# Where the weight steps of one attention turn stand in its written order, and when the last held-back bias rows are stored

## The chip, the cores and the metric

The kernel runs on one core of a Trainium2 chip. The metric is the device time of one execution in microseconds; before the change it is 788.43 us, the median of three runs.

## The reference

Attention with a learned relative-position bias feeds a Fourier mixing layer and a dense layer. Shapes: batch 4, 8 heads, 576 positions, head size 64; model width 512, hidden width 2048.

```python
scores = q @ k.T / sqrt(64) + bias                    # bias: per head, 576 x 576, from a small MLP
attn   = exp(scores - max) / (sum + 1e-9)
x      = concat_heads(attn @ v)                       # [4, 576, 512]
u      = x + real(fft2(x))                            # over positions and width
un     = (u - mean) / sqrt(var + 1e-6)
out    = u + relu(un @ w_ch1) @ w_ch2                 # 512 -> 2048 -> 512
```

## The kernel before

**Stages.** The first stage (about 66 us) computes the bias rows, in 36 steps `u` of 16 rows for all heads, and the scores of attention unit 0. A unit is a pair of heads of one batch element; there are 16. Fifteen turns follow, `turn_of(n, between)` (L530), called from the loop at L579; then a hand-written tail (TAIL, L65), the mixing and the dense layers.

**A turn.** In a turn of about 16 us TensorE computes the scores of unit n while unit n-1 is transposed and multiplied with its values. The order of a turn is written by hand as a list of words (ORDER, L49; SECOND, L57, for n = 1 alone). `S4` is a score block on TensorE (L272), `D4` adds the bias on VectorE and keeps the row extremes (L290), `X4` is the exponential on ScalarE (L298). `T10` and `R1` are transposes on TensorE (L441, L431 to L436), `VT10` and `VR1` copy them from PSUM (L421 on ScalarE or L423 on VectorE), `A0` to `A4` multiply with the values (L462), `Q0` and `Q1` make the reciprocals, `E` and `Y` turn the result back and scale it. A stroke counts back one unit. Turn 0 executes no word, since unit 0 was scored in the first stage and there is no earlier unit. The loop has `tc.manual_schedule` for TensorE, VectorE and ScalarE (L545): these three execute their words in exactly the written order. GpSimd and the DMA queue of SyncE (SP) are ordered by a planner, by program order and by the readiness that it works out for itself.

**PSUM.** Score blocks rotate through 2 buffers (`sps`, L413), so a new `S` waits for the `D` two blocks back. Transposes rotate through 2 buffers (`tps`, L410), so a `T` waits for the copy `V` two transposes back.

**Weight steps.** In every turn from n = 1 on, `weights(n)` (L546) fetches one piece of each dense weight matrix and repacks it from 64-bit float to 32-bit float. The fetches `raw<-m` (L162) are issued on SP as `weights(n)` is called, each when its one buffer is free. Then `W0` and `U0` are ScalarE copies (L164), `W1` to `W3` and `U1` to `U3` are VectorE integer operations (L165 to L167), and behind `W3` and `U3` a store to DRAM is issued on SP (L552, L553). In SECOND these words stand in the second half: `U0` and `W0` ahead of `X6`, `W1` to `W3` behind it, `U1` behind `D8`, `U2 U3` close to the end.

**Held-back rows.** `bias_evac` (L332) writes bias rows into the buffer `ring` and, for every four steps (a group of 64 rows), stores heads 0 and 1 into the tiles that unit 0 reads (L346, L247 to L250). The other six heads go to DRAM by `keep_bias` (L326), six issues at L330, one group later: the list `later` holds back one group while the next is made. `while later: keep_bias()` (L591) stores what is left, at the end of turn 0; by the code that is one group, the last, six issues. Right behind it the tile `x` takes the buffer of `ring` (L593). From turn 3 on the rows come back as `bias<-bias_d` and `bias_r<-bias_d` (L234).

**Other work of a turn.** `prep(n+1)` (L198) splits the next unit's q and k on GpSimd, eight pieces placed behind the words 4, 12, ..., 60 of the list; `load(n+2)` (L183) fetches the unit after it on SP.

```python
rawp, rawu: one buffer "raw" each           # a fetch waits for the last reader of the one before
if len(later) > 1: keep_bias()              # L350, in bias_evac
for i, w in enumerate(SECOND if n == 1 else ORDER):   # L532
```

Of the kernel before, what the change touches and what calls it, by code (L numbers as in the profile page):

```python
# [54 lines left out]


SECOND = """  # L57
S1 D1 S2 T10' D2 S4 T00' VT10' T01' D4 VT00' VT01' S8' S3 T11' VT11' D8' X8' T02' D3 S6 Q0' VT02' D6 S0 R1'
R0' VR1' X3 VR0' D0 S7 S8 U0 T13' T12' W0 A0' D7 X6 W1 VT13' W2 W3 S5 T04' VT12' T03' D8 U1 Q1' A1' X7 X0
VT03' VT04' X1 D5 U2 U3 X5 A2'  # L60
""".split()


# [69 lines left out]
def body(ctx, tc, a, out):  # L133
# [49 lines left out]
    def load(n):  # L183
        hp, b = units[n]
        t = []
        for nm, w in (("qT", 2 * S), ("kT", KW)):
            f = ldp.tile([P, w], F32, tag=nm, name=nm)
            for e in range(2):
                nc.sync.dma_start(f[64 * e:64 * e + 64], a[nm][hp, b])
            t.append(f)  # L190
        ld[n] = t
# [6 lines left out]
    def prep(n):  # L198
        q, k = ld.pop(n)
        qs = stp.tile([P, 2 * S], F32R, tag="qs", name="qs")  # L200
        kh = stp.tile([P, KW], F32R, tag="kh", name="kh")
        kl = stp.tile([P, KW], F32R, tag="kl", name="kl")
        stk[n] = (qs, kh, kl)

        def hi(dst, src, c):
            if n < 2:
                nc.scalar.activation(dst[:, c], src[:, c], AF.Copy)
            else:
                nc.gpsimd.tensor_scalar(dst[:, c], src[:, c], 1.0, 0.0, ALU.mult, ALU.add)  # L209

        def lo(dst, src, ref, rows, c):
            eng = nc.vector if n < 2 else nc.gpsimd
            eng.tensor_tensor(dst[rows, c], src[rows, c], ref[rows, c].bitcast(F32), ALU.subtract)  # L213

        every, low = slice(0, 128), slice(64, 128)
        ca, cb, ck = slice(0, S), slice(S, 2 * S), slice(S, KW)
        return [
            lambda: hi(qs, q, ca), lambda: lo(qs, q, qs, low, ca),
            lambda: hi(kh, k, ca), lambda: lo(kl, k, kh, every, ca),
            lambda: hi(qs, q, cb), lambda: lo(qs, q, qs, low, cb),  # L220
            lambda: hi(kh, k, ck), lambda: lo(kl, k, kh, every, ck),
        ]
# [83 lines left out]
    with ExitStack() as st:  # L306
# [19 lines left out]
        def keep_bias():  # L326

            u, src = later.pop(0)
            for e in range(2, H):
                nc.sync.dma_start(bias_d[4 * (u - 3):4 * (u + 1), e], src[:, e])  # L330
# [74 lines left out]
    with ExitStack() as st:  # L405
# [124 lines left out]
        def turn_of(n, between):  # L530

            for i, w in enumerate(SECOND if n == 1 else ORDER):  # L532
                w, u = w.rstrip("'"), n - w.count("'")
                if w[0] in "WU":
                    if n:
                        wd(w)
                elif 0 <= u < U and (u or n == 1 or w[0] not in "SDX"):
                    steps[w[0]](u, w)
                for piece in between.pop(i, ()):
                    piece()  # L540
            assert not between
# [4 lines left out]
        def weights(n):  # L546

            wf = rawp.tile([P, 512], F32, tag="wf", name="wf")
            uf = rawu.tile([P, DM], F32, tag="wf", name="uf")
            w = widen(a["m1"][:, P * n:P * n + P].rearrange("(k p) c -> p k c", p=P), wf, [P, 4, P], rawp)  # L550
            u = widen(a["m2"][P * n:P * n + P], uf, [P, DM], rawu)
            w.append(lambda: nc.sync.dma_start(w1_d[n].rearrange("p k c -> p (k c)"), wf))  # L552
            u.append(lambda: nc.sync.dma_start(w2_d[n], uf))  # L553

            def step(name):
                todo = w if name[0] == "W" else u
                todo[int(name[1])]()
                if name[1] == "3":
                    todo[4]()
            return step  # L560

        def first_weights(i):

            c = slice(P * (i % 4), P * (i % 4) + P)
            wf = rawx.tile([P, P], F32, tag="wf", name="wx")
            if i < 4:
                res = widen(a["m1"][c, 0:P], wf, [P, P], rawx)
                dst = w1_d[0][:, i]
            else:
                res = widen(a["m2"][0:P, c], wf, [P, P], rawx)  # L570
                dst = w2_d[0][:, c]
            last = res.pop()

            def end():
                last()
                nc.sync.dma_start(dst, wf)
            return res + [end]

        for n in range(U - 1):  # L579
            pr = prep(n + 1) if n else []  # L580
            if n:
                wd = weights(n)
            between = {4 + 8 * i: [piece] for i, piece in enumerate(pr)}
            if n in FIRST:
                for i, piece in zip((10, 30, 40, 50), first_weights(FIRST.index(n))):
                    between[i] = [piece]
            turn_of(n, between)
            if n + 2 < U:
                load(n + 2)
            if n == 0:  # L590
                while later:  # L591
                    keep_bias()
                x = xp.tile([P, B, 5, DM], F32, tag="x", name="x")  # L593
            if n == 6:
                fs = tabp.tile([P, 3, 2, 2, NK], F32R, tag="tab", name="fs")
                nc.gpsimd.tensor_copy(fs[0:1, 0, 0, 0, 0:1], vt[6][0:1, 0, 0:1])
                nc.gpsimd.dma_start(fs, a["fs"])
# [197 lines left out]
        n = U - 1  # L795
# [146 lines left out]
        for b in range(B):  # L942
# [4 lines left out]
            if b + 1 < B:  # L947
                tl, un, pcs = prepare(b + 1)
                n = 4
            else:  # L950
                un, stats, scales = norm(rest_tiles)
                pcs = stats + scales
                n = 2
# [67 lines left out]
```

## Time and profile before

| | |
|---|---|
| three runs | 784.47, 788.43, 788.58 us; median 788.43 |
| the profiled execution | 784.86 us; its span in the trace 783.0 us |
| TensorE busy in the span | 758.1 us (97%) |
| VectorE, ScalarE, GpSimd busy | 433.7, 435.1, 354.1 us |
| mean granted TensorE clock | 0.99 of 2.4 GHz |

Times in the trace count from the first instruction. The second turn (n = 1) lies at 66 to 87 us, the third at 87 to 103 us. A line of a timeline has the start and the duration in us, the engine and the source line, what is written from what is read, and in brackets the idle time just before it with what ended it. Two instructions of one engine can overlap in the records, so the pitch, from one start to the next, is what one costs its engine. In the DMA queue's own timeline (SPq) the duration is that of the issue, not of the transfer.

### The profile page before, as it was taken

To read this page: it belongs to the slowest core of one execution; us is meant where nothing else is said; L and a number is where in the kernel's file an instruction comes from. 1 tells how busy PE (TensorE), PEld (TensorE's weight loads), DVE (VectorE), ACT (ScalarE), POOL (GpSimd) and SP (SyncE) were. 2 spreads that over 40 slices of the span, in tenths; PEclk is the share of its full clock that TensorE was granted. 3 is DMA by queue.
4 is the path that set the end of the run, shared out by engine and by line. 5 is a ranking of instruction groups with operands and counts; after the bars stand their busy time and mean duration, and the time that the engine had idled before them with its cause. 6 is when DMAs were issued, how large, how long until landed. Compare 5 with 4: busy or idle time off the path is not lost.

```text
span 783.0 us, 13209 instructions
## 1 busy us (share of the span) xinstructions
PE 758.1 (97%) x4786; PEld 617.4 (79%) x4786; DVE 433.7 (55%) x958; ACT 435.1 (56%) x898; POOL 354.1 (45%) x299
## 2 busy tenths in 40 slices
PE   6999899999999999979999999999999999999997
PEld 3567678887788877848888888888888888888896
DVE  7996787987877877587471232713237132111433
ACT  7995888788987888434333333334333342333453
POOL 0003556554663644256554434644355444445442
PEclk9999999999999999979999999999999999999999
DMA  8988989989879743631211121112211112111321
GB/s 220 238 222 228 254 235 297 298 227 283 243 204 284 204 135 92 208 110 28 66 32 50 43 94 54 40 41 64 72 54 41 41 54 95 43 53 54 119 90 61
DMA packets 59488, 103.16 MB, mean 132 GB/s; under 512 B 8768, under 2 KB 28864, under 8 KB 58304
## 3 DMA queue, kind: packets, MB, share of 16 engines
q1 hardware_dynamic: 58672, 98.99, 44.1%
q0 software_dynamic: 288, 3.02, 1.2%
q8 instruction: 37, 0.61, 0.3%
q10 hardware_dynamic: 464, 0.33, 0.1%
q14 instruction: 27, 0.22, 0.1%
HBM read 78.58 MB, written 21.07 MB: 127 GB/s over the span
## 4 chain that ended last, share of the span: by engine, by line
PE 88%; DVE 3%; ACT 3%; DMA 3%; SPq 2%; issue 1%; ACTq 0%; DVEq 0%
PE hp L898 25%; PE acc L912 25%; PE s L272 10%; PE o L462 10%; PE t L441 7%; PE bps L391 4%; PE zp L674 2%; PE abp L693 2%; DMA raw<-m 2%; SPq L330 1%; ACT p L298 1%; PE t L493 1%; DVE un L773 1%; PE ut L787 1%; PE t L431 1%
## 5 line engine op out<-in xcount | busy, mean ns | idle before, releaser
L904 DVE SCALAR_TENSOR_TENSOR hl<-hp,hh 128x512 fp32r<-128x512 f32 (+1 forms) x80 | 50.9, 636 | 229.4 <-ACT hh L903 229.4
L878 POOL TENSOR_TENSOR w1l<-w,w1h 128x512 fp32r<-128x512 f32 x80 | 105.8, 1323 | 106.1 <-ACT w1h L877 104.9
L878 POOL TENSOR_TENSOR w2l<-w2f,w2h 128x512 fp32r<-128x512 f32 x64 | 85.2, 1331 | 102.8 <-ACT w2h L877 102.5
L877 ACT ACTIVATE w1h<-w 128x512 fp32r<-128x512 f32 x80 | 50.4, 632 | 125.6 <-PE hp L898 110.2
L898 PE MATMUL hp<-uh,w1h 128*128 128x512 f32 (+1 forms) x320 | 118.7, 372 | 0.8 <-ACT uh L789 0.8
L898 PE MATMUL hp<-ul,w1h 128*128 128x512 f32 (+1 forms) x320 | 118.7, 371 | 0.7 <-DVE ul L790 0.7
L898 PE MATMUL hp<-uh,w1l 128*128 128x512 f32 (+1 forms) x320 | 118.5, 370 | 0.0
L290 DVE CUSTOM_DVE_ANT_0 p<-s,bias 128x576 f32<-128x576 f32 x128 | 95.1, 754 | 38.8 <-PE s L272 35.3
L877 ACT ACTIVATE w2h<-w2f 128x512 fp32r<-128x512 f32 x80 | 50.6, 632 | 117.8 <-POOL w1l L878 76.3
L912 PE MATMUL acc<-w2l,hh 128*128 128x512 f32 x288 | 112.4, 390 | 0.0
L912 PE MATMUL acc<-w2h,hh 128*128 128x512 f32 x288 | 111.9, 391 | 0.0
L912 PE MATMUL acc<-w2h,hl 128*128 128x512 f32 x288 | 107.4, 391 | 0.0
L272 PE MATMUL s<-kh,qs 128*128 128x288 f32 (+1 forms) x320 | 98.6, 327 | 1.9 <-DVE nm L290 1.8
L298 ACT ACTIVATE p<-p,nm 128x576 f32<-128x576 f32 x128 | 98.0, 772 | 2.8 <-DVE nm L290 1.6
L421 ACT ACTIVATE pt<-t 128x512 f32<-128x512 f32 x141 | 77.9, 594 | 35.9 <-PE t L441 20.0
L272 PE MATMUL s<-kl,qs 128*128 128x288 f32 (+1 forms) x320 | 88.2, 295 | 0.8 <-DVE kl L213 0.8
L462 PE MATMUL o<-pt,v 128*64 128x288 f32 x640 | 85.3, 412 | 0.0
L441 PE MATMUL t<-ident,p 128*128 128x128 f32 x576 | 80.4, 276 | 3.9 <-ACT pt L421 3.7
L209 POOL TENSOR_SCALAR kh<-kT 128x576 fp32r<-128x576 f32 (+1 forms) x28 | 22.8, 831 | 134.6 <-PE s L272 113.5
L272 PEld LDWEIGHTS s<-kh,qs 128*128 128x128 f32 (+1 forms) x320 | 58.4, 183 | 18.7 <-issue 7.0
L441 PEld LDWEIGHTS t<-ident,p 128*128 128x128 f32 x576 | 67.0, 142 | 7.3 <-ACT pt L421 4.8
L898 PEld LDWEIGHTS hp<-ul,w1h 128*128 128x128 f32 x320 | 60.8, 190 | 11.7 <-DVE ul L790 1.5
(136 smaller groups left out, 1387.1 us busy)
## 6 DMA issues: line engine op xcount, KB each, us to landing
w2f<-w_d SPq DMA_DIRECT2D x80, 256.0 KB, 2.6
raw<-m SPq DMA_DIRECT2D x30, 512.0 KB, 5.3
kT<-kT SPq DMA_DIRECT2D x32, 304.0 KB, 4.8
qT<-qT SPq DMA_DIRECT2D x32, 288.0 KB, 4.6
bias_d<-ring SPq DMA_DIRECT2D x54, 144.0 KB, 2.7
bias<-bias_d SPq DMA_DIRECT2D x24, 288.0 KB, 5.4
v<-v SPq DMA_DIRECT2D x16, 320.0 KB, 6.3
out<-x SPq DMA_DIRECT2D x18, 256.0 KB, 2.7
```

The lines of the kernel that those rows point to most:

```text
L272: nc.tensor.matmul(ps[:m, c, :CH], qs[:, c0:c0 + m], kk[:, k0 + c * CH:k0 + (c + 1) * CH], start=k == 0, stop=k == 1, skip_group_check=True)
L290: nc.vector.tensor_tensor_reduce(p, bank.pop((n, i))[:, :, :CH], bias, -0.125, 3.0e38, ALU.add, ALU.min, nms[n][:, blk:blk + 1])
L298: nc.scalar.activation(p, p, AF.Exp, bias=nms[n][:, blk:blk + 1], scale=-1.0, accum_out=sums[n][:, blk:blk + 1])
L391: nc.tensor.matmul(ps[32 * t4:32 * t4 + 32, c, :CH], w2[:, int(rev)], h[:, c * CH:(c + 1) * CH], start=True, stop=True, tile_position=(0, ...
L421: nc.scalar.activation(dst, src, AF.Copy)
L441: nc.tensor.transpose(tp[:, 128 * t:128 * t + 128], pb[t].rearrange("p h s -> p (h s)")[:, k0:k0 + 128], ident)
L462: nc.tensor.matmul(os_[u][e, c, :CH], vt[u][:, j, e], pts[u][:, 2 * j + h if j < 4 else 8, c * CH:(c + 1) * CH], start=j == 0, stop=j == 4 ...
L877: nc.scalar.activation(h, src, AF.Copy)
L878: eng.tensor_tensor(l, src, h.bitcast(F32), ALU.subtract)
L898: nc.tensor.matmul(ps[:, :N], (wh, wl)[wi][:, P * kb:P * kb + P], ut[ui][:, kb, :N], start=i == 0, stop=i == len(mm) - 1)
L904: nc.vector.scalar_tensor_tensor(hl[:, :N], ps[:, :N], 0.0, hh[:, :N].bitcast(F32), ALU.max, ALU.subtract)
L912: nc.tensor.matmul(acc[t], h[i][:, P * t:P * t + P], w[j], start=f == 0 and k == 0, stop=f == NF - 1 and k == 2)
```

## The change

Two edits. In SECOND the words W0 to W3 and U0 to U3 move to the end of the list, in the order W0 U0 W1 W2 W3 U1 U2 U3; all other words keep their order and the list its length of 62. The words W and U of ORDER, which all later turns use, stay. The second edit stores the held-back bias rows, and allocates `x`, at the end of turn 1, behind `load(3)`, and no longer at the end of turn 0.

```diff
 SECOND = """
-S1 D1 S2 T10' D2 S4 T00' VT10' T01' D4 VT00' VT01' S8' S3 T11' VT11' D8' X8' T02' D3 S6 Q0' VT02' D6 S0 R1'
-R0' VR1' X3 VR0' D0 S7 S8 U0 T13' T12' W0 A0' D7 X6 W1 VT13' W2 W3 S5 T04' VT12' T03' D8 U1 Q1' A1' X7 X0
-VT03' VT04' X1 D5 U2 U3 X5 A2'
+S1 D1 S2 T10' D2 S4 T00' VT10' T01' D4 VT00' VT01' S8' S3 T11' VT11' D8' X8' T02' D3 S6 Q0' VT02' D6 S0 R1' R0'
+VR1' X3 VR0' D0 S7 S8 T13' T12' A0' D7 X6 VT13' S5 T04' VT12' T03' D8 Q1' A1' X7 X0 VT03' VT04' X1 D5 X5 A2' W0
+U0 W1 W2 W3 U1 U2 U3
 """.split()
...
             if n + 2 < U:
                 load(n + 2)
-            if n == 0:
+            if n == 1:
                 while later:
                     keep_bias()
                 x = xp.tile([P, B, 5, DM], F32, tag="x", name="x")
```

## Rows read from the trace of the kernel before

**Rows 1.** The page: its first line, and the busy times of TensorE (with its weight loads), VectorE, ScalarE and GpSimd.
```profile
span 783.0 us, 13209 instructions
PE 758.1 (97%) x4786; PEld 617.4 (79%) x4786; DVE 433.7 (55%) x958; ACT 435.1 (56%) x898; POOL 354.1 (45%) x299
```

**Rows 2.** Who waited for whom on TensorE from 60 to 380 us, the row of the transposes: us in total, times, longest.
```profile
PE t L441 <- ACT pt L421: 3.7, 3, 2.9
```

**Rows 3.** The chain of waits from 55 to 122 us: start, us, what. The fetch of the weights, the copy that it releases, the value products of the second turn and third turn's first transposes.
```profile
74.02 5.49 DMA raw<-m
...
79.53 0.66 ACT uf L164
...
83.18 4.03 PE o L462 x32
...
89.65 0.44 PE t L441 x4
```

**Rows 4.** TensorE's timeline: T13' and T12' of the second turn, its T04' and T03', and T04' and T03' of the third turn.
```profile
76.23 1.04 PE L441 MATMUL t<-ident,p 128*128 128x128 f32 x8
...
82.03 1.14 PE L441 MATMUL t<-ident,p 128*128 128x128 f32 x8 [2.91 <-ACT pt L421]
...
97.79 1.04 PE L441 MATMUL t<-ident,p 128*128 128x128 f32 x8
```

**Rows 5.** ScalarE's timeline: VR0', U0, W0, then VT03' with VT04', and X8' of the third turn's list (behind X1 and X5); last U0, and VT13' with VT12', of the third turn.
```profile
74.68 0.60 ACT L421 ACTIVATE pt<-t 128x512 f32<-128x512 f32 x1 [0.32 <-PE t L431]
79.53 0.66 ACT L164 ACTIVATE uf<-raw 128x512 f32<-128x512 f32 x1 [4.25 <-DMA raw<-m]
80.09 0.65 ACT L164 ACTIVATE wf<-raw 128x512 f32<-128x512 f32 x1
...
83.87 1.08 ACT L421 ACTIVATE pt<-t 128x512 f32<-128x512 f32 x2
...
86.34 0.78 ACT L298 ACTIVATE p<-p,nm 128x576 f32<-128x576 f32 x1
...
94.27 0.65 ACT L164 ACTIVATE uf<-raw 128x512 f32<-128x512 f32 x1
...
96.16 1.07 ACT L421 ACTIVATE pt<-t 128x512 f32<-128x512 f32 x2
```

**Rows 6.** The SP queue's timeline: a bias row load of the fourth turn, the last stores of bias rows (two rows, 12 issues), the second turn's weight fetches, another early load, the store behind U3 and the third turn's fetch for U.
```profile
60.36 0.59 SPq L239 DMA_DIRECT2D bias<-bias_d  x1
...
62.76 4.22 SPq L330 DMA_DIRECT2D bias_d<-ring  x5
...
68.96 4.38 SPq L330 DMA_DIRECT2D bias_d<-ring  x7
73.46 1.12 SPq L162 DMA_DIRECT2D raw<-m  x2
74.62 0.55 SPq L247 DMA_DIRECT2D bias_r<-bias_d  x1
...
86.67 0.33 SPq L553 DMA_DIRECT2D w_d<-uf  x1
87.05 0.43 SPq L162 DMA_DIRECT2D raw<-m  x1
```

**Rows 7.** VectorE's timeline: W1, the D8 behind W3, U2, U3, and then D1 and VR1' of the third turn; last U1 and U3 of the third turn.
```profile
80.77 0.43 DVE L165 TENSOR_SCALAR raw<-raw 128x512 int32<-128x512 int32 x1 [4.61 <-ACT wf L164]
...
82.57 0.75 DVE L290 CUSTOM_DVE_ANT_0 p<-s,bias 128x576 f32<-128x576 f32 x1
...
84.85 0.69 DVE L166 SCALAR_TENSOR_TENSOR raw<-raw 128x512 int32<-128x512 int32 x1
85.58 1.07 DVE L167 SCALAR_TENSOR_TENSOR uf<-uf,raw 128x512 int32<-128x512 int32 x1
87.97 0.76 DVE L290 CUSTOM_DVE_ANT_0 p<-s,bias 128x576 f32<-128x576 f32 x1 [1.32 <-PE s L272]
...
88.66 0.45 DVE L423 COPY pt<-t 64x64 f32<-64x64 f32 x2
...
98.17 0.75 DVE L165 TENSOR_SCALAR raw<-raw 128x512 int32<-128x512 int32 x1
...
100.22 1.04 DVE L167 SCALAR_TENSOR_TENSOR uf<-uf,raw 128x512 int32<-128x512 int32 x1
```

**Rows 8.** GpSimd's timeline: the last pieces of `prep(2)`, and the first pieces of `prep(3)`.
```profile
76.58 2.78 POOL L213 TENSOR_TENSOR qs<-qT,qs 64x576 fp32r<-64x576 f32 x2
84.89 2.35 POOL L209 TENSOR_SCALAR kh<-kT 128x576 fp32r<-128x576 f32 x2 [5.53 <-DMA kT<-kT]
87.21 1.43 POOL L213 TENSOR_TENSOR kl<-kT,kh 128x576 fp32r<-128x576 f32 x1
```

**Rows 9.** The instructions on the tile `raw` in the whole span: ns min/median/max, first and last start, forms; and the time from the issue of a fetch to its landing.
```profile
L165 DVE TENSOR_SCALAR raw<-raw x38: 224/428/1030, 80.8 to 315.1; 128x512 int32<-128x512 int32 x30, 128x128 int32<-128x128 int32 x8
L166 DVE SCALAR_TENSOR_TENSOR raw<-raw x38: 277/693/1942, 81.2 to 317.5; 128x512 int32<-128x512 int32 x30, 128x128 int32<-128x128 int32 x8
...
L167 DVE SCALAR_TENSOR_TENSOR uf<-uf,raw x15: 691/702/1157, 85.6 to 318.2; 128x512 int32<-128x512 int32 x15
...
DMA to landing us min/median/max: 3.4/5.2/8.3
```

## The prediction

> **What bounds the kernel now.** The page comes first: TensorE is busy for 758.1 of 783.0 us [rows 1], so only a stretch in which it stands still can be shortened by a new order. The list of TensorE's waits says where one is: between 60 and 380 us the transposes waited three times for ScalarE's copies, 3.7 us in all, 2.9 us of it at once [rows 2]. TensorE's timeline puts that wait at T04' of the second turn, at 82.03 us, after 2.91 us idle [rows 4]. The chain of waits tells why: a weight fetch landed 5.49 us after 74.02 and released U0 on ScalarE [rows 3]. ScalarE had been idle for 4.25 us in front of U0, although VT13', for which T04' waits, stood behind it with its input ready: T13' and T12' ended by 77.27 [rows 4, 5]. The fetch was late because its issue, at 73.46, stood behind twelve stores of bias rows on SP [rows 6]. So the change aims at one place, and that place holds 2.91 us, 0.37% of the profiled execution.
>
> **Part 1, the words W and U at the end of SECOND.** What goes: U0 and W0 no longer stand in front of X6 and VT13'. ScalarE is free from 75.28 (74.68 + 0.60), does X6, and has both copies done before 78.1 (77.27 and two copies, 1.08 as a pair) [rows 4, 5]. TensorE reaches T04' at 79.12 (82.03 - 2.91), so nothing holds it there: minus 2.91 us at this point. The score buffers don't hold it either, because D7 and D8 no longer have a weight step ahead of them; `prep(2)` ends at 79.36 (76.58 + 2.78) [rows 8], some 5 us before its first use.
>
> What comes late next is VectorE, and here most of the gain is lost. Work forward from T04' at 79.12:
> - T04' and T03' take 1.14, to 80.26; ScalarE's VT03' then starts there and not at 83.87 [rows 5], 3.61 earlier. From VT03' to the end of X5 ScalarE has no gap (83.87 to 86.34), so X5 ends at 82.73. W0 starts there, U0 0.56 later (79.53 to 80.09), both done by 83.9.
> - On VectorE W1 starts 0.68 after W0 does (80.09 to 80.77), at 83.41. Three steps take 1.80 (W1 at 80.77, D8 behind W3 at 82.57) [rows 5, 7]; six take 3.60, to 87.01. D1 of the third turn stands behind them in the same queue, and VR1' behind D1: 0.69 (87.97 to 88.66) and 0.45. VR1' ends at 88.15.
> - T10' of the third turn needs the PSUM buffer that VR1' empties. In the chain of before it starts at 89.65, and from 82.03 to there TensorE is never idle [rows 3, 4]. It would be ready 2.91 earlier, at 86.74, but has to wait for 88.15. The gain left is 89.65 - 88.15 = 1.50 us; 1.4 us of standing still has moved over the turn's border.
>
> One term more: U1 to U3 now run at 85.2 to 87.0, beside the first pieces of `prep(3)`, on GpSimd from 84.89 [rows 8]. The nearest rows are the same steps beside such pieces. In the second turn U3 took 1.07 and not the 0.69 of the fastest; in the third, U1 took 0.75 where the median is 0.43, and U3 1.04 [rows 7, 9]. I charge U1 and U3, 0.32 + 0.35 = 0.67, since U2 kept its 0.69 in the second turn. What stands is a gain of 0.8 us. Bounds: if VectorE does not hold T10' at all, 2.9 us gained; with all six steps at the longest durations of the whole trace, 2 x (1.03 + 1.94 + 1.16) = 8.3 and not 3.6, 4.7 more, it is 3.2 us slower. I take the value near rows 7, because these are the same instructions beside the same GpSimd pieces; the longest ones are of some other stretch.
>
> The Trainium skill, page "SBUF — State Buffer", has a rule on which operations interfere: VectorE and GpSimd share one port pair as an exclusive lock, and the loser of a VectorE operation with two SBUF inputs and a GpSimd operation fully blocks. By it each of U1 to U3 could wait for a whole GpSimd operation. The trace so far shows 0.3 to 0.4 us lost at a meeting, less than a whole piece.
>
> The DMAs that move with these words: the stores behind W3 and U3, and with them the third turn's fetches, since each has one buffer. The fetch for U was issued at 87.05, 0.4 after U3 ended at 86.65 [rows 6, 7]. U3 now ends near 87.7, so the issue falls at 88.1; with the median landing of 5.2 [rows 9] the data is there at 93.3. The third turn's U0 stood at 94.27 without a wait [rows 5], and comes 0.8 earlier, at 93.5. That just fits: cost nothing, cover 0.2 us. Past that there is TensorE's own cover: T04' of the third turn needs VT13', started at 96.16, done by 96.7, and runs at 97.79 [rows 4, 5], which leaves 1.1 us more. The two small transfers behind Q1' leave SP earlier than before; nothing waits there. On GpSimd nothing is moved past: the same `prep(2)` pieces in the same sequence.
>
> **Part 2, the held-back rows.** The list holds one group by the code, not two, so six issues of 0.63 us (4.38 for seven) move, 3.8 us of SP time. The planner fills SP with what is ready: loads for the fourth turn stand at 60.36 and 74.62, far ahead of their place in the program [rows 6]. The held rows are ready when the first stage ends. So I expect the two fetches at about 69.6, behind the seventh store, with the six stores directly behind them, before 74.62. The fetches would land by 75.6 (5.5 each), but their first reader is W0 at 82.7: with part 1 in place an issue at 73.46, landing at 79.5, is early enough as well. So part 2 is worth nothing beside part 1; by itself, with the words where they were, it would have removed most of the 2.91 us. Bounds: 0, or 3.8 us of SP time if the stores come in front of the third turn's fetches.
>
> **The sum.** 784.86 (span 783.0 and 1.9 around it) - 0.8 + 0 = 784.1. The timed runs lie at two levels: one at 784.47, like the profiled execution, and two at 788.4 to 788.6. The median is of the upper level, 3.6 above the profiled one. I carry the difference over: 788.4 - 0.8 = 787.6 us.
>
> **Rivals.**
> - The wait comes back one turn later: the third turn's U0 waits for its fetch. From an issue at 88.1 it decides once the landing takes over 6.5 us (5.4 to U0, 1.1 to TensorE); the longest landing is 8.3 [rows 9], a stall of 1.8 and a net loss of 1.0: 785.9 in the profile, 789.4 as a median. Stores issued in front of it would do the same at 5.2. For it: the cover is only 0.2 + 1.1. Against it: the median, and the early loads of rows 6. This is the slower side.
> - VectorE's steps are blocked by whole GpSimd pieces: U1 to U3 wait out two pieces of kh and one of kl, 2.35 + 1.43 = 3.8 us [rows 8] in place of 0.67. T10' then starts at 91.9, 2.3 later than before: 787.1, or 790.7. Against it, rows 7. It is what the lock would do on the page "SBUF — State Buffer" of the Trainium skill.
> - VectorE holds nobody, because the six steps end by 85.6 (86.74 less D1 and VR1', 1.14): the full 2.9, 782.0 or 785.5. Against it: W1 can't start before W0, and six steps at 0.6 take 3.6.
> - The upper level is itself this wait: the executions at 788.5 would be those in which the fetch of rows 3 lands some 4 us later, as its range to 8.3 partly allows. Then the wait goes in all runs, and the median comes down to 784. For it: this fetch ends the longest of TensorE's waits on ScalarE. Against it: only an execution of the lower level is profiled, and other transfers could do it too.
> - Nothing changes (a gain of 0.3 or less), because some fetch or store further back sets the pace. Against it: TensorE leads the chain.
>
> **How the numbers follow.** Forecast, a gain of 0.3 to 1.5: 0.50. Wait one turn later 0.13, GpSimd 0.06, full gain 0.07, upper level gone 0.16, nothing 0.08. A difference of 0.5%, 3.9 us, is about what can be told from no change here, as the runs themselves spread over 4.1 us. No mechanism but the fourth rival moves the time by that much; the level on which the next median falls does. One of three runs was at the lower level, so a median there has a chance of about a quarter, and 784.5 - 0.8 = 783.7 then counts as faster. Together (0.16, and nearly a quarter of the rest that gains) 0.30 for faster; slower by that much needs a loss no rival reaches, 0.06; 0.64 for neither. The range goes from the lower level with the full gain, 784.5 - 2.9 = 781.6, to the upper level with the late fetch, 789.6.
>
> **What would show it.** Right: no wait of ScalarE in front of U0, T04' of the second turn near 79.1 without idle time, W0 near 82.7, six steps on VectorE in one piece to about 87.7, T10' of the third turn behind an idle time of 1.4 to 2.1 us that ends with VR1', the fetches at about 69.6. Wrong: an idle time in front of the third turn's U0 that reaches T04'; T10' without a wait; the stores issued behind 82 us; or a new difference behind 104 us, where no step of this working lies.

## The result: 0.63% slower, because a fetch of the third turn comes 6 us later

| | before | after |
|---|---|---|
| median of 8 runs each | 788.10 us | 792.01 us |
| lowest, highest | 784.47, 788.95 | 790.21, 794.37 |
| ratio after / before, of the means | | 1.0063 (95%: 1.0043 to 1.0083) |
| the profiled execution, its span | 784.86, 783.0 | 790.21, 788.4 |
| mean granted TensorE clock | 0.99 | 0.991 |

The page of after, its first line and its busy times, against [rows 1]:

```profile
span 788.4 us, 13208 instructions
...
PE 758.5 (96%) x4786; PEld 616.1 (78%) x4786; DVE 436.4 (55%) x958; ACT 434.8 (55%) x898; POOL 355.6 (45%) x299
```

The span grew by 5.4 us and TensorE's busy time by only 0.4. Who waited for whom on TensorE, 60 to 380 us, against [rows 2]:

```profile
PE t L441 <- ACT pt L421: 5.7, 3, 4.5
```

The same kind of wait, now 4.5 us at once in place of 2.9. TensorE's timeline of after says where, against [rows 4]; T04' of the second turn, T10', T13' and T04' of the third:

```profile
79.30 1.03 PE L441 MATMUL t<-ident,p 128*128 128x128 f32 x8
...
87.71 0.66 PE L441 MATMUL t<-ident,p 128*128 128x128 f32 x4 [0.90 <-ACT pt L421]
...
93.85 1.04 PE L441 MATMUL t<-ident,p 128*128 128x128 f32 x8
...
101.23 1.82 PE L441 MATMUL t<-ident,p 128*128 128x128 f32 x8 [4.49 <-ACT pt L421]
```

T04' of the second turn runs 2.73 us earlier and without idle time (82.03 before). T13' of the third turn is still 1.20 us ahead (95.05 before). Then T04' of the third turn is 3.44 us behind (97.79 before). ScalarE's timeline, against [rows 5], has the reason one step up: W0 and U0 of the second turn run where the order puts them, and U0 of the third waits 5.57 us for its fetch.

```profile
82.86 0.67 ACT L164 ACTIVATE wf<-raw 128x512 f32<-128x512 f32 x1
83.43 0.68 ACT L164 ACTIVATE uf<-raw 128x512 f32<-128x512 f32 x1
...
98.73 0.66 ACT L164 ACTIVATE uf<-raw 128x512 f32<-128x512 f32 x1 [5.57 <-DMA raw<-m]
```

The SP queue's timeline, against [rows 6]: the second turn's two fetches, the held-back stores, the store and fetch of W, then k of unit 4, and only then the store and fetch of U.

```profile
69.98 1.13 SPq L162 DMA_DIRECT2D raw<-m  x2
71.16 3.73 SPq L330 DMA_DIRECT2D bias_d<-ring  x6
...
85.48 0.34 SPq L552 DMA_DIRECT2D w_d<-wf  x1
85.86 0.43 SPq L162 DMA_DIRECT2D raw<-m  x1
91.40 1.11 SPq L189 DMA_DIRECT2D kT<-kT  x2
92.57 0.58 SPq L553 DMA_DIRECT2D w_d<-uf  x1
93.19 0.43 SPq L162 DMA_DIRECT2D raw<-m  x1
```

VectorE's timeline, against [rows 7]: W1, U3, D1 of the third turn, VR1'.

```profile
83.56 0.44 DVE L165 TENSOR_SCALAR raw<-raw 128x512 int32<-128x512 int32 x1 [3.30 <-ACT wf L164]
...
86.55 0.69 DVE L167 SCALAR_TENSOR_TENSOR uf<-uf,raw 128x512 int32<-128x512 int32 x1
87.16 0.75 DVE L290 CUSTOM_DVE_ANT_0 p<-s,bias 128x576 f32<-128x576 f32 x1
...
87.84 0.45 DVE L423 COPY pt<-t 64x64 f32<-64x64 f32 x2
```

Read the last two views together. U3 is done by 87.24, so its store could go out there. It goes out at 92.57, because the two transfers of unit 4's kT load stand in front of it, and they wait for their buffer; SP's own waits name the reader that keeps it, GpSimd's kl of unit 3:

```profile
SPq L189 <- POOL kl L213: 4.9, 1, 4.9
```

```profile
88.44 2.94 POOL L213 TENSOR_TENSOR kl<-kT,kh 128x576 fp32r<-128x576 f32 x2
```

The fetch, behind the store since it reuses the buffer that U1 to U3 read, is issued at 93.19 where it was 87.05 before: 6.14 us later. In the kernel before, the same load waited for the same reader (kl, 87.21 to 90.16), but it was issued behind the fetch and out of its way:

```profile
87.21 2.95 POOL L213 TENSOR_TENSOR kl<-kT,kh 128x576 fp32r<-128x576 f32 x2
```

```profile
90.18 1.14 SPq L189 DMA_DIRECT2D kT<-kT  x2
```

Two more lines of after say what T10' of the third turn waited for. It started at 87.71, as VR0' ended on ScalarE and before VR1' began on VectorE (87.84). VectorE's steps held TensorE only at the second score block behind it:

```profile
87.07 0.59 ACT L421 ACTIVATE pt<-t 128x512 f32<-128x512 f32 x1
```

```profile
89.14 0.40 PE L272 MATMUL s<-kh,qs 128*128 128x288 f32 x1 [0.25 <-DVE nm L290]
```

The chain of waits of after leads from the fetch to TensorE, against [rows 3], and the windows show the clock:

```profile
93.19 5.52 DMA raw<-m
...
101.23 1.82 PE t L441 x8
103.05 4.93 PE o L462 x32
```

```profile
97.00:99.00 2.00, 0.00 (x0) 0.00 (x0) 0.00 (x0) 0.27 (x1) 1.12 (x2) 1.00 1.09 279
...
101.00:103.00 2.00, 1.77 (x10) 1.44 (x10) 1.97 (x5) 2.00 (x6) 1.59 (x3) 0.61 0.21 62
103.00:105.00 2.00, 2.00 (x11) 1.08 (x12) 2.00 (x4) 2.00 (x7) 2.00 (x3) 0.54 0.85 238
```

(Columns: stretch, its length, the busy time of TensorE, its weight loads, VectorE, ScalarE, GpSimd, then the granted clock, the DMA share, GB/s.) Behind the 4.49 us of idle time the granted clock is 0.61 and 0.54, near the lower level of 1.2 GHz. The eight transposes take 1.82 us and not 1.04, the 32 value products 4.93 and not the 4.03 of [rows 3]: 1.68 us more. 3.44 and 1.68 make 5.12; the next marker, the transpose of L493, stands at 108.55 against 103.42, 5.13 later. Nothing is won or lost on balance from there on: the last unit's first transposes stand at 326.26 against 320.91, 5.35 later, and the end 5.4 later.

### The profile page after: what moved, and what is told of

The parts are those of the page before. It is cut to its first block, busy times and chain, and to the rows that moved or that the text cites. A ratio compares the mean times of both kernels' runs of the same rounds, so it can differ in the third digit from the quotient of the medians.

```text
span 788.4 us, 13208 instructions
## 1 busy us (share of the span) xinstructions
PE 758.5 (96%) x4786; PEld 616.1 (78%) x4786; DVE 436.4 (55%) x958; ACT 434.8 (55%) x898; POOL 355.6 (45%) x299
## 4 chain that ended last, share of the span: by engine, by line
PE 83%; DVE 8%; DMA 4%; ACT 3%; issue 2%; ACTq 0%; DVEq 0%; SPq 0%
PE acc L912 24%; PE hp L898 24%; PE s L272 10%; PE o L462 8%; PE t L441 7%; PE bps L391 3%; PE abp L693 2%; PE zp L674 2%; DMA raw<-m 1%; ACT p L298 1%; DMA bias<-ring 1%; DVE un L773 1%; PE ut L787 1%; PE t L431 1%; DMA kT<-kT 1%
## 5 line engine op out<-in xcount | busy, mean ns | idle before, releaser
L209 POOL TENSOR_SCALAR kh<-kT 128x576 fp32r<-128x576 f32 (+1 forms) x28 | 21.8, 797 | 142.2 <-PE s L272 121.6
L898 PEld LDWEIGHTS hp<-uh,w1h 128*128 128x128 f32 x320 | 60.7, 190 | 12.9 <-DVE hl L904 1.7
```

The costliest lines, as they stand in the source:

```text
L898: nc.tensor.matmul(ps[:, :N], (wh, wl)[wi][:, P * kb:P * kb + P], ut[ui][:, kb, :N], start=i == 0, stop=i == len(mm) - 1)
```

## Experiments

The theory is **the place in SP's queue**: with U3 last, the load of kT is issued on SP ahead of the store and fetch of U, and it waits for GpSimd. The rivals are **the six stores** of the second edit, **the DMA engines full** with other transfers, and **VectorE's lump** of six steps. Ratios are to the kernel before, timed beside it.

**Each edit alone, and both with one load moved.** The words alone:

```diff
-R0' ... S8 U0 T13' T12' W0 A0' D7 X6 W1 VT13' W2 W3 ... D8 U1 ... D5 U2 U3 X5 A2'
+R0' ... S8 T13' T12' A0' D7 X6 VT13' ... D8 ... D5 X5 A2' W0 U0 W1 W2 W3 U1 U2 U3
```

> Only the words W and U at the end of SECOND; the held rows are stored after turn 0 as before. My theory: the loss comes from the third turn's fetch for U, which the SP queue now holds behind the kT load of unit 4, so it does not need the second edit: as slow as the full change, 3 to 6 us over before, an idle time of 4 to 5 us in front of T04' of the third turn, while T04' of the second runs at about 79. Rival (the stores of the held rows, now behind the fetches, do the harm): 1 us faster than before and no such idle time.

Measured: 792.30 us, 1.0059 (1.0037 to 1.0081): the whole loss. In its SP timeline kT stands in front again:

```profile
91.32 1.11 SPq L189 DMA_DIRECT2D kT<-kT  x2
92.48 0.58 SPq L553 DMA_DIRECT2D w_d<-uf  x1
93.10 0.43 SPq L162 DMA_DIRECT2D raw<-m  x1
```

TensorE then stands still for 4.11 us in front of T04', which starts at 101.43. The stores of the second edit are not needed for the loss.

The rows alone:

```diff
-            if n == 0:
+            if n == 1:
                 while later: keep_bias()
```

> Only the held rows behind the second turn; the words stand as before. My theory: the two fetches of the second turn go out at about 70 and land at 75.5, so U0 waits for nothing, T04' of the second turn loses its 2.9 us of idle time and VectorE has no lump of steps to hold T10': 2.5 to 3 us faster than before, and the third turn's U0 does not wait. Rival (the early fetches only push other transfers back, kT of unit 3 above all): no difference within 1 us.

Measured: 789.18, 1.0025 (1.0003 to 1.0047): the gain failed to come. The second turn's U0 does start without a wait, at 77.18, but W2 and W3 now run beside GpSimd's pieces, for 1.79 and 1.80 us; and in the fifth turn T04' waits 2.38 us for a fetch issued at 123.84 (120.74 before).

Both edits, with the load of unit 4 issued on GpSimd's queue:

```diff
-                nc.sync.dma_start(f[64 * e:64 * e + 64], a[nm][hp, b])
+                (nc.gpsimd if n == 4 else nc.sync).dma_start(f[64 * e:64 * e + 64], a[nm][hp, b])
```

> Both edits, and the four transfers of load(4) issued from the GpSimd queue and not from SP. My theory: the store behind U3 and the third turn's fetch for U are then issued at about 87.7 and not at 93.2, land at about 93, and the third turn's U0 waits for at most 0.5 us: the 4.5 us idle time in front of T04' goes, with the lower clock behind it, and the kernel is 0.5 to 1.8 us faster than before. Rival (the fetch is late because U3 itself ends later, whatever stands in front of it on SP): the idle time stays at 3 us or more and the kernel is as slow as the full change, 3 to 6 us over before.

Measured: 788.96, 1.0012 (0.9993 to 1.0031). With kT out of the queue the store goes out at 88.88, right behind U3 (87.08 and 1.78), the fetch at 89.26, and T04' of the third turn has no idle time: that stall is gone, and the loss with it.

```profile
88.88 0.33 SPq L553 DMA_DIRECT2D w_d<-uf  x1
89.26 0.42 SPq L162 DMA_DIRECT2D raw<-m  x1
```

```profile
99.80 1.04 PE L441 MATMUL t<-ident,p 128*128 128x128 f32 x8
```

A gain isn't there either, and VectorE's timeline says why:

```profile
85.03 0.90 DVE L165 TENSOR_SCALAR raw<-raw 128x512 int32<-128x512 int32 x1
85.96 1.08 DVE L166 SCALAR_TENSOR_TENSOR raw<-raw 128x512 int32<-128x512 int32 x1
87.08 1.78 DVE L167 SCALAR_TENSOR_TENSOR uf<-uf,raw 128x512 int32<-128x512 int32 x1
```

U1 to U3 take 3.76 us and not 1.80, beside GpSimd's kh (from 84.77) and kl (from 86.48). TensorE pays with 0.90, 1.55 and 0.38 us of idle time between 86 and 91 us, the last two behind VectorE, and with a granted clock of 0.74, 0.50 and 0.91 in the three stretches of 2 us from 90 on. T13' of the third turn stands at 97.07, 2.0 us behind the kernel before. Here the second rival of the prediction stands, which in the trace of after is absent only because kh started at 86.66 there.

**The same lump, U ahead of W.** If kT is issued in front of whichever store comes last, it must now delay W's fetch.

```diff
-... X5 A2' W0 U0 W1 W2 W3 U1 U2 U3
+... X5 A2' U0 W0 U1 U2 U3 W1 W2 W3
```

> Both edits, with the last words of SECOND in the order U0 W0 U1 U2 U3 W1 W2 W3. My theory: whichever store comes last is planned behind kT of unit 4, so now the fetch for W goes out at about 93 and the third turn's W0, which stands directly behind U0 on ScalarE, waits for it: the same loss, 3 to 6 us over before. Rival (the loss belongs to U's own buffer or its longer steps): no idle time in front of T04' of the third turn, 1 us faster than before.

Measured: 792.22, 1.0053 (1.0031 to 1.0074).

```profile
86.73 0.34 SPq L553 DMA_DIRECT2D w_d<-uf  x1
...
92.35 1.11 SPq L189 DMA_DIRECT2D kT<-kT  x2
93.52 0.58 SPq L552 DMA_DIRECT2D w_d<-wf  x1
94.14 0.43 SPq L162 DMA_DIRECT2D raw<-m  x1
```

Now W is behind kT, and it is W0 that waits, for 4.3 us. So the place in the queue decides, and not which matrix it is.

**The words in the middle.** Both copies behind X0 and the six steps behind D5, early enough for U's store to pass ahead of kT; the rows first as before, then held back:

```diff
-... D8 U1 Q1' A1' X7 X0 VT03' VT04' X1 D5 U2 U3 X5 A2'
+... D8 Q1' A1' X7 X0 U0 W0 D5 W1 VT03' W2 W3 VT04' U1 X1 U2 U3 X5 A2'
```

> The held rows after turn 0 as before; in SECOND the copies U0 W0 stand behind X0, and W1 to W3 and U1 to U3 behind D5, not at the end. My theory (a late fetch costs only what stands behind its copy, and a store that ends late lets kT of unit 4 in front on SP): U0 finds its data at 79.5, T04' runs at about 79 without idle time, the six steps end by 84.5, before D1 of the third turn is due, and the stores keep their place in front of kT of unit 4, so the third turn's U0 does not wait: 2 to 3 us faster than before. Rival (what is gained early is lost again in the turns in which the SP queue and the transfers are full): within 1 us of before or slower, with a wait of ScalarE for a fetch in turns 4 to 9.

> The same order of SECOND with the held rows behind the second turn. My theory: the fetch is early enough in both, so the second edit adds nothing: within 1 us of the run with the words alone in the middle. Rival (the held rows, now behind the fetches, make the first loads of bias rows wait on SP for their landing, about 1.2 us, and everything behind them on SP runs later): 1 to 3 us slower than that run.

Measured: 786.78, 0.9994 (0.9974 to 1.0013), and with the rows held back 788.79, 1.0026 (1.0009 to 1.0042). In the first there is no wait of a transpose from 60 to 200 us, U's store goes out at 87.88 and kT at 91.38; the expected 2 to 3 us are still not in the time. The rows cost some 2 us; in that trace the third turn's fetches, issued at 84.61 and 86.56, land after 6.5 and 8.8 us, and T04' waits 2.48 us.

**Two more ways around the queue.** The rows alone with the load of unit 3 on GpSimd's queue (the line of the third kernel with `n == 3`), and both edits with the third turn's words at its end too:

```diff
+THIRD = [w for w in ORDER if w[0] not in "WU"] + "W0 U0 W1 W2 W3 U1 U2 U3".split()
-            for i, w in enumerate(SECOND if n == 1 else ORDER):
+            for i, w in enumerate(SECOND if n == 1 else THIRD if n == 2 else ORDER):
```

> The held rows behind the second turn, the words as before, and the four transfers of load(3) issued from the GpSimd queue. My theory for the loss of the rows-only run: its qT of unit 3 was issued at 84 to 86 and not at 79.6, each prep and each load behind it then ran late by 2 to 3 us, and so the fifth turn's fetch for U waited on SP until 123.8. With load(3) off SP the wait of the fifth turn goes and the early gain stays: 1.5 to 3 us faster than before. Rival (the gain is lost to the landing times of full queues, whoever issues): still 1 to 3 us slower than before, with a wait of ScalarE for a fetch in some turn from 4 to 9.

> Both edits, and in the third turn too the words W and U at the end of the list; the SP queue still has kT of unit 4 in front of the store behind U3. My theory: the third turn's copies now stand behind T04' and its copies, so the fetch that lands at 98.7 holds nobody there; T04' of the third turn runs at about 97 without idle time and the clock stays up. The fourth turn then begins behind a lump of six steps (1 to 2 us), and its own fetches are late. Within 1.5 us of before if its U0 finds its data, 3 to 6 us over if the same wait only moves into the fourth turn. Rival (the third turn is slow for another reason than the waiting copy): the idle time in front of T04' of the third turn stays at 4 us.

Measured: 788.13, 1.0018 (0.9992 to 1.0045), its lead of 3 us at the second turn lost in pieces of 1.15, 1.06 and 1.92 us of waiting, in front of T04' of the third, fifth and ninth turn. And 798.15, 1.0147 (1.0116 to 1.0178): the third turn's late fetch holds nobody now (T04' at 99.76, no wait, 2.0 us behind the kernel before, since U1 to U3 took 3.76 us beside GpSimd as with the load moved), but the lump moves the stall one turn on, and GpSimd stretches it; W1 to W3 of the third turn:

```profile
104.03 1.73 DVE L167 TENSOR_SCALAR raw<-raw 128x512 int32<-128x512 int32 x1 [3.30 <-ACT wf L166]
105.78 1.80 DVE L168 SCALAR_TENSOR_TENSOR raw<-raw 128x512 int32<-128x512 int32 x1
107.62 1.77 DVE L169 SCALAR_TENSOR_TENSOR wf<-wf,raw 128x512 int32<-128x512 int32 x1
```

Six steps take 7.1 us and not 3.6, and the fourth turn opens with 5.25 us of idle time on TensorE.

**Half the bytes.** From the third turn's fetches on each weight fetch leaves out half the rows, and the stores write the other half twice, so that only the bytes fetched change: in the kernel before, in the two with the words in the middle, and in the changed kernel.

```diff
+            q = P if n < 2 else 64
-            u = widen(a["m2"][P * n:P * n + P], uf, [P, DM], rawu)
+            u = widen(a["m2"][P * n:P * n + q], uf[:q], [P, DM], rawu, q)
```

> The kernel before, with half of each dense weight fetch left out from the third turn's fetches on (64 of 128 rows; the store writes these rows twice, so stores and engine work stay). Control for the next two. My theory (in turns 3 to 9 the landing of fetches in full DMA engines takes back any lead of TensorE): the second turn's fetch is whole, so its wait stays; the small waits behind it go: 0 to 1.5 us faster than before. Rival (the pace is set by the issue order on SP alone, not by bytes): the same as before within 0.5 us.

> The words in the middle (copies behind X0, six steps behind D5), held rows as before, with the same half of the fetches left out. My theory: no wait for a fetch in any turn, so the second turn's gain reaches the end: 2 to 3.5 us faster than before. Rival (the lead is not lost in fetches; the median execution simply has no wait in the second turn to remove, because its first stage ends later): no faster than the halved kernel before, within 0.7 us.

> The words in the middle and the held rows behind the second turn, with the same half of the fetches left out. My theory: the 2 us that the held rows cost with whole fetches come from a longer landing of the third turn's fetches (6.5 to 8.8 us in that profile, against 4.7 to 6.4) and so go: within 0.7 us of the halved kernel with the words alone in the middle. Rival (the cost is the order on SP: the loads of bias rows wait there for the held rows to land): still 1.5 to 2.5 us slower than that one.

> Both edits, with the same half of the fetches left out. My theory: the third turn's fetch for U is still issued at about 93, behind kT of unit 4, and lands 4 us later and not 5.5: the idle time in front of T04' of the third turn falls from 4.5 to about 3 us, and 1 to 3 us over before remain. Rival (the full landing time, not the place on SP, makes that wait): the idle time falls under 1 us and the kernel is no slower than before.

Measured, in that order: 1.0003 (0.9979 to 1.0027), 0.9999 (0.9975 to 1.0022), 0.9994 (0.9970 to 1.0017), 1.0055 (1.0031 to 1.0079). The changed kernel is as slow as with all the bytes: its U fetch still stands behind kT (92.16) and goes out at 93.95. But it is a weak test of the DMA engines, because the halved fetch still landed after 5.2 us (5.52 whole), and not after 4 as expected. T04' of the third turn starts at 101.68:

```profile
101.68 1.14 PE L441 MATMUL t<-ident,p 128*128 128x128 f32 x8 [1.23 <-ACT pt L421]
```

The idle time in front of it is 1.23 us and not the expected 3, since TensorE had lost the difference before: it stood still for 0.91, 0.34 and 0.38 us between 88 and 92, and its granted clock was 0.50 from 92 to 94. That the place on SP makes the stall therefore rests on the load moved, on U ahead of W, and on the landing in after itself, 5.52 us where the median of before is 5.2 [rows 9]; not on this run.

The 2 us that the held-back rows cost beside the words in the middle don't show with half the bytes (0.9994 against 0.9999), and the wait in front of T04' of the third turn is 0.58 us there and not 2.48. That points to transfers; the ratios alone, each uncertain by some 2 us, don't show it. The words in the middle show no gain with half the bytes either, though their trace still has waits of 0.82 and 1.63 us, at 127.95 and 155.27.

**Where the 2.9 us went.** One question is left: a wait of 2.9 us was in the trace, and kernels without it are no faster. Two more traces of the kernel before and two of the words in the middle, each a single execution:

> The kernel before, traced a second time. Theory (a), a late first stage covers the wait: if S8 of the second turn starts at 77.5 us or later (75.63 in the first trace), the idle time in front of T04' is under 1 us, and the products A1' of the second turn still start at 83 to 84 us. Theory (b), the wait is there each time: idle time of 2.3 to 3.5 us in front of T04' wherever S8 stands, A1' at 83 plus whatever the first stage is late.

> The kernel before, traced a third time; the same as for the second. By the rival that the upper level of the runs (788.5) is this wait grown longer, an execution near 788 us would show a wait of 6 us or more here; by the theories (a) and (b) the 3 to 4 us between the levels stand elsewhere, in the turns 4 to 9 or behind 330 us.

> The words in the middle, traced a second time. Neither theory has a wait in front of T04' of the second turn. Theory (b): S8 near 75.7 and A1' near 80.1, 3 us ahead of the kernel before, and the lead is gone by the tenth turn (196 us, within 1 us of the kernel before), through new waits of 0.5 to 2 us in the turns 4 to 9. Theory (a): where S8 is at 77.5 or later, A1' is level with the kernel before.

> The words in the middle, traced a third time; the same as for the second. If a lead of 2 us or more lasts to 330 us while the execution is no faster, neither theory holds, and the difference stands in the tail or in the dense layers.

The executions took 788.00, 793.06, 789.60 and 787.26 us. With the earlier traces, in us (the kernel with half the bytes and the old order is the kernel before up to the third turn's fetches, and so is its counterpart with the words in the middle):

| order | S8 of the second turn starts | T04' starts | idle time before it |
|---|---|---|---|
| before | 75.63, 75.80, 76.25, 77.11 | 82.03, 81.64, 81.77, 81.84 | 2.91, 2.35, 2.02, 1.24 |
| words in the middle | 75.82, 76.56, 78.07, 78.76 | 79.15, 79.89, 81.41, 82.10 | none |

Before, T04' starts at 81.6 to 82.0 wherever S8 stands: U0's fetch sets it. Without that wait it starts 3.33 us behind S8, and S8 depends on the end of the first stage. The two rows of the kernel before, its second trace, as TensorE's timeline has them:

```profile
77.11 0.37 PE L272 MATMUL s<-kh,qs 128*128 128x288 f32 x1 [0.47 <-DVE nm L290]
...
81.84 1.14 PE L441 MATMUL t<-ident,p 128*128 128x128 f32 x8 [1.24 <-ACT pt L421]
```

So the wait is a cushion that takes up a late first stage; theory (a) holds, only with a wait that shrinks and does not vanish. Over the eight traces S8 stands at 76.75 on average; 3.33 behind that is 80.1, and so what can be won is, by this estimate, 81.8 less 80.1, 1.7 us, not 2.9.

Part of that goes back later, as theory (b) has it. The kernel with the words in the middle and an early S8 (76.56) is 2.07 us ahead of the kernel before at A1' of the second turn (80.85 against 82.92 in the second trace; 0.55 of it is the earlier S8), and 0.31 ahead at A1' of the fifth (130.75 against 131.06). ScalarE and TensorE in between, in the fifth turn of that kernel:

```profile
127.17 0.67 ACT L164 ACTIVATE uf<-raw 128x512 f32<-128x512 f32 x1 [2.34 <-DMA raw<-m]
```

```profile
129.68 1.14 PE L441 MATMUL t<-ident,p 128*128 128x128 f32 x8 [1.48 <-ACT pt L421]
```

U0 of the fifth turn starts at 127.17 here and at 127.36 in the first trace of before, though A1' of the fourth turn stood at 112.58 here and at 114.85 there: both fetches go out at 120.7, behind the loads of bias rows on SP. In the kernel before it is nearly in time: its U0 waits 0.79 us, its T04' does not. It is a second such stop, and a lead ends there. The third trace of the kernel before, the execution of 793.06 us, shows it grown: there the same fetch goes out at 122.10, U0 starts at 130.54, and TensorE pays the price of after once more:

```profile
133.05 1.97 PE L441 MATMUL t<-ident,p 128*128 128x128 f32 x8 [3.24 <-ACT pt L421]
134.95 6.20 PE L462 MATMUL o<-pt,v 128*64 128x288 f32 x32
```

The next transposes of L435 stand at 142.16 there and at 136.17 in the second trace; the spans end 3.9 us apart (790.0 and 786.1).

The 3.1 us between 784.86 and 788.00 stand elsewhere: 0.46 up to the last unit's first transposes (320.91 and 321.37), 1.46 more up to the mixing's first L787 (341.90 and 343.82), 1.2 behind that. No wait in the second turn does it.

What stays open: the ratio of the words in the middle, 0.9994, is bounded by 0.9974, some 2 us, so a gain of the few tenths that are left after both effects can't be told from none. No order tried was measurably faster than the kernel before.

## Why the prediction was wrong

**Part 1, ScalarE, TensorE and VectorE: right up to VR1', wrong on what T10' waits for.** No wait of ScalarE in front of the second turn's U0; T04' at 79.30 (79.12 forecast), W0 at 82.86 (82.73), U3 done at 87.24 (87.7 with the charge for GpSimd, 87.0 without), VR1' done at 88.29 (88.15). T10' of the third turn was to wait 1.4 us (2.1 with the charge) for the buffer that VR1' empties. It waited 0.90 us, for VR0' on ScalarE, and started before VR1' did: at 87.71 and 87.84, with the words alone at 87.94 and 88.42, with the load moved at 87.38 and 89.45. So that step of the prediction doesn't hold in these kernels, nor does the rule, stated for PSUM above, that a T waits for the copy two transposes back; why T10' may start so early the traces don't show. VectorE's steps hold the score blocks behind it, for 0.25 us in after. The gain that was left where T13' of the third turn starts is 1.20 us, inside the forecast of 0.3 to 1.5, but by another way, and with the luck that kh started at 86.66 and not at 84.89. A small sum is off too: both copies are done by 78.35 (77.27 and 1.08), not before 78.1; T04' at 79.12 is later still.

**Part 1, "The DMAs that move with these words ... cost nothing, cover 0.2 us": the step that failed.** The issue of the fetch for U was put at 88.1, 0.4 us behind U3, as in [rows 6]. It came at 93.19, behind kT of unit 4, and cost 4.49 us of idle time and 1.68 of slower clock. That step looked at what the fetch needs (U3 done, the buffer free) and not at which DMAs can stand in front of it in the queue of an engine that issues in order. Part 2 used [rows 6] to show that the planner brings loads forward; this step did not. That kT could come ahead of a moved store was a case to ask for, and the trace of before had the row for its price: kT of unit 4 was issued at 90.18 there, right behind the end of GpSimd's kl (87.21 and 2.95). The sentence on the two small transfers behind Q1', "nothing waits there", failed as well: in after they went out at 79.97, between the two halves of unit 3's kT load, whose second half followed at 81.20; before, both halves were out by 78.96.

**The first rival had the place and the order of waits** (third turn's U0, then T04'), and its last sentence the cause: "Stores issued in front of it would do the same". Its price was wrong twice. The time of the issue was kept at 88.1, so that only a long landing (8.3) could hurt; the landing was ordinary, 5.52. And the clock was left out: of the 5.13 us lost, 1.68 are the slower clock behind the idle time. By the trace of before alone, kT out at 91.3 (90.18 and 1.14), a store of 0.33 and the median landing of 5.2 put the data at 96.9; in the rival's own terms (U0 due at 93.5, a cover of 1.1) that is a stall of 2.3 us with an ordinary landing, not 1.8 with the longest, and a net loss of 1.5 before the clock. Of the other 2.2 us, 1.2 came from GpSimd, whose kl ended later than before (91.38 against 90.16); the rest is made up of a landing of 5.52, a store of 0.58, and TensorE being 1.20 ahead and not 0.8.

**Part 2, "worth nothing beside part 1": not refuted beside these words** (words alone 1.0059, both edits 1.0063), but not in general: beside the words in the middle the held-back rows cost 2 us. The fetches went out at 69.98 as forecast (69.6).

**The GpSimd rival:** absent in after, present in full with the load of unit 4 moved (U3 1.78 us beside kl) and in the kernel with the third turn's lump (1.73 to 1.80 for each of three steps). The charge of 0.32 to 0.35 us for a meeting fits the pieces of L209 (kh), beside which a step took 0.3 to 0.5 us more (U3 1.03 with the words alone; U1 0.90 and U2 1.08 with the load moved). It is too small for the pieces of L213 (kl), beside which U3 took 1.1 us more; the prediction used one price for both. The trace of before had the row: the longest L166 of [rows 9], 1.94 us, starts at 147.85 beside a kl piece (147.82 to 149.24), and the prediction set it aside as "of some other stretch". The rival's own 3.8 us was too large: with the load moved U1 to U3 took 1.96 us more than alone. The rule of the Trainium skill, page "SBUF — State Buffer", section "Who interferes with whom", that the loser of such a meeting fully blocks, is nearer to the rows of L213 than the charge taken from [rows 7].

**The fourth rival, that the upper level of the runs is this wait grown, falls:** with executions of 788.00 and 793.06 us the wait was 1.24 and 2.02, smaller and not larger.

## What to carry to other kernels

Moving a step that ends in a DMA moves that DMA's place in the queue: list what else is ready to be issued there, and price a blocked transfer in front of it, not only the data it waits for. A wait seen in one trace may be a cushion: ask what sets its end and what sets its beginning, and how much the beginning varies from execution to execution, before it is booked as a gain. A stall of TensorE is priced with the slower clock that may follow it: 1.68 us behind 4.49 here, none behind the 2.91 of [rows 4].

## What the runs showed of the hardware

- The granted clock after idle time of TensorE: 4.49 us left 0.61 and 0.54 in the two stretches behind it, and cost 1.68 us on top; 3.24 us did the same (32 value products 6.20 us). In the kernel with words in the middle and rows held back, 2.48 us were followed by a mean of 0.87 over 97 to 110 us, while the 2.91 us of [rows 4] left T04' at 1.14 us, with the products behind it at full speed. With the load moved, waits of 0.90, 1.55 and 0.38 us were followed by 0.50 from 92 to 94 us, and with half the bytes waits of 0.91, 0.34 and 0.38 by the same. The length of one idle time doesn't tell which.
- VectorE's integer steps that read two tiles (L166, L167) take 0.69 us alone, 0.7 to 1.2 beside a GpSimd piece that reads one tile (L209), and 1.2 to 1.9 beside one that reads two (L213), up to three in a row (the kernel before in three traces, after, and nine others, 76 to 150 us). It hits the step that reads one tile (L165) too: 0.42 us alone, up to 0.9 beside L209, 1.73 beside L213 in the kernel with the third turn's lump. In after U3 kept its 0.69 beside kh, and kh took 1.80 us for two pieces in place of 1.36.
- A fetch of 512 KB landed after 5.2 us in the median of before [rows 9], but after 8.4 for the fifth turn's fetch in the third trace of the kernel before (6.6 in the first, with the same four loads of bias rows ahead of it), and after 8.8 with the words in the middle and the rows held back.
